# First batch of an attention + FFN kernel: plain value casts and plain products ahead of the dilated scores, a quarter of w_in in three loads, and a new order for the third FFN tile's first products

## The chip, the cores and the metric

One core of one Trainium2 chip. The metric is the device time of one launch in microseconds (us), as the median over runs. The engines that the text speaks of are PE (TensorE: matmuls, with its weight loads shown as PEld), DVE (VectorE), ACT (ScalarE), POOL (GpSimd, which here mostly issues loads) and SP (SyncE, which issues loads, transposing transfers and stores).

## The reference

Two stages. Attention over 8 batches, 8 heads, 576 tokens and head size 64, in which heads 0 to 3 ("plain") see the last 32 tokens, and heads 4 to 7 ("dilated") see every fourth token of the last 128:

```python
scores = scale * np.matmul(q, k.transpose(0, 1, 3, 2))
mask_plain = (rel >= 0) & (rel < window)
mask_dil = (rel >= 0) & (rel < window * dilation) & (rel % dilation == 0)
attn = np.exp(scores); attn = attn / (np.sum(attn, axis=-1, keepdims=True) + 1e-09)
attn_out = np.matmul(attn, v)
```

Then a feed-forward network on the 4608 tokens, each a row of 512 (8 heads x 64):

```python
h = np.maximum(x @ w_in, 0.0)          # 512 -> 2048
out = h * h @ w_out                    # 2048 -> 512
```

## The kernel before

**Tiling.** Heads go in pairs e = 0 to 3; pairs 0 and 1 are plain, 2 and 3 dilated. Tokens are kept by residue modulo 4. The attention's result goes, transposed and in bf16, into a ring `xT` (partitions: 128 of the 512 features, so four k-blocks `kt`, one for each head pair). The FFN takes tokens in tiles of 512; the first two tiles are made as four half tiles of 256. In a tile the first layer accumulates in PSUM over the four k-blocks (`mm1`, L971), ScalarE takes the relu (L984), VectorE squares (L987); the second layer (`g2`, L1026) multiplies by `w_out`. A half tile's accumulator holds two of the sixteen blocks of 128 hidden features, a full tile's one. The pool `ps_f` has four PSUM buffers, shared by the first layer's accumulators, the second layer's outputs and some scores.

**What orders the work.** Nothing is scheduled by a planner: each engine runs its instructions in the order in which the program issues them, and waits where its operands or its buffer aren't ready. That order is written out by hand in the string `PROGRAM`. Its first part, up to the first `|`, runs ahead of the FFN; each later part runs after one FFN group (`ffn_groups` gives the groups, `g1` those of the first layer). For batch 0, part 0 (the first 256 tokens) and part 1 (the other 320) of pair e, a code is a letter, e and the part:

- `T` PE transposes q and k into PSUM (L794), `C` copies them to SBUF, on ACT for a code that ends in a, else on DVE (L801 for dilated pairs, with a second copy at L803 for part 1; L808 and L809 for plain ones)
- `B` puts the mask's bias into PSUM (L824), `S` the scores (L846), `E` the exponential on ACT (L854), in part 1 with a mask multiplied in on DVE (L857)
- `P` products with the values (L884), `D` the sums that normalise (L900), `L` and `X` their reciprocal as log and exponential on ACT (L907, L910), `M` the division into `xT` on DVE (L917). In part 0 L, X and M take both pairs at once: L00, X00, M00 for the plain ones, L20, X20, M20 for the dilated
- `w` and `W` are zero products (`turn`, L764) of 512 and 256 columns, which keep PE running while it would wait; `w1+31` is one that adds into S31's accumulator
- `N` zeroes halves of the values' tile `vbd` on DVE (L1047, L1048); `h` casts the plain values of the first four blocks of 64 tokens from float32 into it on DVE (L1139; SP loads them at the start, L1065); `j` casts the dilated tail (L1142); `G` spreads dilated values into `vbd` (L245); `u` makes masks on ACT
- `L0:i0` loads a quarter of w_in, `L0:i1a` and `L0:i1b` halves of the second quarter (k-blocks 0 and 1, 2 and 3), `L0:v1s` and `L0:v1t` plain values of part 1, `L0:o0` to `o3` w_out: all issued on POOL's queue

**POOL's queue.** Its loads share eight semaphores in turn, so each waits, ahead of its issue, until the load eight before it has landed.

**The FFN's first groups.** In the first half tile a group of `g1` covers two accumulators and two k-blocks: group 0 and 1 use w_in's first quarter, 2 and 3 its second. The dilated pairs' `xT` blocks (k-blocks 2 and 3) are first read in group 1. In the third tile (tokens 1024 to 1535) the k-blocks come in the order 2, 3, 1, 0, and the first four groups issue the sixteen products of the first four accumulators in an order of their own.

Of the kernel before, what the change touches and what calls it, by code (L numbers as in the profile page):

```python
# [18 lines left out]


PROGRAM = (
# [42 lines left out]
def kernel(  # L64
# [29 lines left out]
    NT = 512  # L94
# [7 lines left out]
    KT = DM // P  # L102
# [826 lines left out]
    def store(osb, pos: int, c0: int, c1: int, cuts=None):  # L929

        x = 0
        while x < P:
            b, y = divmod(pos + x, S)
            part = int(y >= RES * MN[0]) if b in PARTED else 0
            w = MN[part] if b in PARTED else M
            r, m = divmod(y - RES * MS[part], w)
            n = min(P - x, w - m)
            row = b * S + RES * (MS[part] + m) + r
            at = cuts(n) if cuts else (c0, c1)
            for y0, y1 in zip(at, at[1:]):  # L940
                nc.sync.dma_start(out[row : row + RES * (n - 1) + 1 : RES, y0:y1], osb[x : x + n, y0:y1])
            x += n

    def ffn_groups(tk0: int, nt: int):

        early = NT <= tk0 <= 3 * NT
        h2 = h2_pool.tile([P, NF, NT], bf16, name="h2T")
        per = NT // nt  # L950
        kts = (2, 0, 3, 1) if tk0 > 3 * NT else (2, 3, 1, 0) if tk0 == 2 * NT else (0, 1, 2, 3) if tk0 == 0 else (2, 3, 0, 1)
        cur, acc = {}, {}

        half = nt // 2
        over = tk0 // RING != (tk0 + nt - 1) // RING
        assert not over or (tk0 + half) % RING == 0

        def mm1(u, ks):
            if u not in acc:
                acc[u] = ps_f.tile([P, NT], f32, name="pf")  # L960
            for x in range(per):
                f = per * u + x
                piece = max(y for y in range(len(w_in_sb)) if w_cuts[y] <= P * f)
                c0 = 512 * (f // 4) + f % 4 - w_cuts[piece]
                for kt in ks:
                    t0 = tk0 % RING
                    to, rhs = acc[u][:, nt * x : nt * x + nt], xT[:, kt, t0 : min(t0 + nt, RING)]
                    if over:
                        to = to.rearrange("p (a t) -> p a t", a=2)
                        rhs = xT[:, kt, :].rearrange("p (a t) -> p a t", t=half)[:, 0 : t0 // half + 1 : t0 // half, :]  # L970
                    nc.tensor.matmul(  # L971
                        to,
                        w_in_sb[piece][:, kt, c0 : c0 + 509 : 4],
                        rhs,
                        start=(kt == kts[0] and x == 0),
                        stop=(kt == kts[-1] and x == per - 1),
                        skip_group_check=True,
                    )
            if ks[-1] != kts[-1]:
                return  # L980
            hv = h2[:, per * u : per * u + per, 0:nt]

            def relu():
                nc.scalar.activation(hv, acc[u][:, :].rearrange("p (x n) -> p x n", x=per), ACT.Relu)  # L984

            def square():
                nc.vector.tensor_tensor(out=hv, in0=hv, in1=hv, op=ALU.mult)  # L987

            def floor():
                nc.vector.tensor_scalar(  # L990
                    out=hv, in0=acc[u][:, :].rearrange("p (x n) -> p x n", x=per), scalar1=0.0, scalar2=None, op0=ALU.max
                )

            if tk0 == 0 and u < 2:
                held.append((floor if u else relu, square))
            else:
                relu()
                square()

        def g1(i):  # L1000
            if i < 2 and tk0 < NT or i < 6 and tk0 == 0:
                x, y = divmod(i, 2)
                for ks in [kts[2:3], kts[3:]] if tk0 and y else [kts[2 * y : 2 * y + 2]]:
                    for u in (2 * x, 2 * x + 1):
                        mm1(u, ks)
            elif i < 2 and early:
                for u in (2 * i, 2 * i + 1):
                    mm1(u, kts[:2])
            elif i < 4 and tk0 == 2 * NT:
                for u, x in ((0, 2), (1, 2), (2, 2), (0, 3)) if i == 2 else ((1, 3), (3, 2), (2, 3), (3, 3)):  # L1010
                    mm1(u, kts[x : x + 1])
            elif i < 4 and early:
                for u in (2 * i - 4, 2 * i - 3):
                    mm1(u, kts[2:])
            else:
                mm1(i, kts)

        def g2(m, part):
            last = tk0 + P * (m + 1) == NTOK
            if part == 0 or last and part == 2:  # L1020
                cur[m] = ps_f.tile([P, DM], f32, name="pf")

            c0, c1 = ((0, 384), (384, DM))[part // 2] if last else (0, DM)
            f0, f1 = (NF // 2 * (part % 2), NF // 2 * (part % 2 + 1)) if last else (4 * part, 4 * part + 4)
            for f in range(f0, f1):
                nc.tensor.matmul(  # L1026
                    cur[m][:, c0:c1], h2[:, f, P * m : P * m + P], w_out_sb[:, f, c0:c1],
                    start=(f == 0), stop=(f == NF - 1),
                )
            if f1 == NF:  # L1030
                osb = osb_pool.tile([P, DM], f32, name="osb")
                (nc.vector.tensor_copy if last and part == 1 or tk0 == 3 * NT // 2 else nc.scalar.copy)(osb[:, c0:c1], cur[m][:, c0:c1])  # L1032
                pos = tk0 + (P * m + half) % nt if over else tk0 + P * m
                if tk0 == NTOK - NT and m in (0, 2):
                    store(osb, pos, c0, c1, lambda n: (c0, DM // 2, c1) if m == 0 or n > P // 2 else (c0, c1))
                else:
                    store(osb, pos, c0, c1)

        return [lambda i=i: g1(i) for i in range(NF // per)] + [
            lambda m=m, part=part: g2(m, part) for m in range(nt // P) for part in range(4)  # L1040
        ]
# [58 lines left out]

    def load_w_in(x, half=""):

        ks = {"": slice(0, KT), "a": slice(0, KT // 2), "b": slice(KT // 2, KT)}[half]
        nc.gpsimd.dma_start(
            w_in_sb[x][:, ks, :],
            moe_w_in[P * ks.start : P * ks.stop, w_cuts[x] : w_cuts[x + 1]].rearrange("(kt p) f -> p kt f", p=P),
        )
# [191 lines left out]
```

## Time and profile before

| | |
|---|---|
| median of 3 runs | 296.63 us (296.29 to 296.87) |
| the profiled execution | 296.3 us, span 294.3 us |
| PE busy | 289.2 us, 98% of the span |
| ACT, DVE, POOL busy | 64%, 53%, 42% |
| granted TensorE clock | 0.998 |

The span runs from the first to the last instruction in the trace; 2.0 us of the profiled time lie outside it. Rows of a timeline give the start in us from the span's start, the time from the first instruction's start to the last one's end, engine, line, operation, what is written and read, shapes, and how many instructions are merged in the row; in brackets the idle time before it and what ended that. A matmul's end is modelled and overlaps with the next one's start, so distances between starts are the better measure. A row of the table by stretches gives the stretch, its length, then for PE, PEld, DVE, ACT and POOL the busy time and the number of instructions, then granted clock, DMA share and GB/s.

### The profile page before, as it was taken

Reading aid. Unit: us, or ns where it says so; the run is one execution under the profiler, and the core shown is the slowest. Engines: PE = TensorE matmul, PEld = TensorE weight load, DVE = VectorE, ACT = ScalarE, POOL = GpSimd, SP = SyncE. Lnnn points to the kernel's source line nnn. Section 1 sums busy time; section 2 is a strip of 40 time slices with the busy share of each in tenths; the row PEclk is TensorE's granted clock in tenths of the full one; section 3 lists DMA queues with packets and bytes.
Section 4 is the critical chain, followed back from the end, with each engine's and each line's share of the span. In section 5 each row is a group of like instructions: output and inputs, shape, how many; then the busy total and the mean of one; then the engine's idle time right before and its main releaser. Section 6 shows DMA issues by size and latency. Waiting matters only on the chain.

```text
span 294.3 us, 7986 instructions
## 1 busy us (share of the span) xinstructions
PE 289.2 (98%) x3273; PEld 167.0 (57%) x3273; DVE 155.1 (53%) x449; ACT 187.7 (64%) x382; POOL 123.2 (42%) x208
## 2 busy tenths in 40 slices
PE   8999999999999999999999999999999999999995
PEld 7689647859555554555455545554554455445443
DVE  2786225646669666785659465947454244004400
ACT  6888635887767774988577656766676466127511
POOL 8676266666647959365873688000000000000000
PEclk9999999999999999999999999999999999999999
DMA  8999999999999999989999699012101210121022
GB/s 120 196 185 210 205 217 195 176 178 171 177 219 145 142 203 165 129 134 167 171 175 137 91 146 174 7 36 74 36 2 39 72 38 0 36 74 36 0 71 74
DMA packets 82996, 35.48 MB, mean 121 GB/s; under 512 B 52384, under 2 KB 78208, under 8 KB 82960
## 3 DMA queue, kind: packets, MB, share of 16 engines
q0 software_dynamic: 49056, 18.49, 56.6%
q1 hardware_dynamic: 33760, 16.38, 28.0%
q8 instruction: 26, 0.43, 0.6%
q10 hardware_dynamic: 144, 0.10, 0.1%
q14 instruction: 10, 0.08, 0.1%
HBM read 37.50 MB, written 9.44 MB: 159 GB/s over the span
## 4 chain that ended last, share of the span: by engine, by line
PE 98%; ACT 0%; issue 0%; DVE 0%; ACTq 0%
PE pf L1026 43%; PE pf L971 43%; PE po L764 2%; PE po L369 2%; PE pa L369 1%; PE pf L369 1%; PE pa L794 1%; PE pd L369 1%; PE pf L846 1%; PE pa L564 0%; PE po L884 0%; PE pf L824 0%; PE pd L900 0%; PE pf L564 0%; PE pf L884 0%
## 5 line engine op out<-in xcount | busy, mean ns | idle before, releaser
L971 PE MATMUL pf<-xT,w_in 128*128 128x512 bf16 (+1 forms) x704 | 127.9, 341 | 0.0
L1026 PE MATMUL pf<-w_out_sb,h2T 128*128 128x512 bf16 (+2 forms) x592 | 127.8, 373 | 0.0
L984 ACT ACTIVATE h2T<-pf 128x512 bf16<-128x512 f32 x143 | 83.9, 600 | 32.2 <-PE pf L971 31.9
L971 PEld LDWEIGHTS <-w_in 128*128 128x128 bf16 x704 | 78.0, 113 | 46.3 <-issue 0.3
L987 DVE TENSOR_TENSOR h2T<-h2T 128x512 bf16<-128x512 bf16 x144 | 60.1, 424 | 62.6 <-ACT h2T L984 60.5
L1026 PEld LDWEIGHTS <-h2T 128*128 128x128 bf16 x592 | 56.1, 98 | 63.9
L323 POOL DMA_DIRECT2D vbd<-in_v_dram x80 | 43.6, 553 | 22.8 <-DMA qb<-in_q_dram 8.6
L1032 ACT COPY osb<-pf 128x512 f32<-128x512 f32 (+1 forms) x34 | 19.5, 574 | 50.5 <-PE pf L1026 50.5
L173 POOL DMA_DIRECT2D qb<-in_q_dram x19 | 13.6, 720 | 10.4 <-DMA xx<-qb 7.3
L713 ACT ACTIVATE rec<-rec 128x576 f32<-128x576 f32 x24 | 16.4, 682 | 0.7
L173 POOL DMA_DIRECT2D kb<-in_k_dram x19 | 13.3, 699 | 6.0 <-DMA vd<-in_v_dram 1.8
L195 POOL DMA_DIRECT2D vbd<-in_v_dram x16 | 10.9, 679 | 10.6 <-DMA kb<-in_k_dram 4.8
L730 ACT ACTIVATE pt<-pa 128x384 bf16<-128x384 f32 (+1 forms) x26 | 11.7, 498 | 4.7 <-DVE xT L720 3.8
L309 POOL DMA_DIRECT2D vd<-in_v_dram x20 | 12.0, 614 | 2.7 <-DMA vbd<-in_v_dram 1.6
L716 DVE TENSOR_TENSOR xT<-pf,rec 128x512 bf16<-128x512 f32 x11 | 7.6, 692 | 10.5 <-ACT rec L713 10.5
L315 POOL DMA_DIRECT2D vbd<-in_v_dram x20 | 12.0, 622 | 1.6 <-PE pf L369 1.6
L716 DVE TENSOR_TENSOR xT<-po,rec 128x512 bf16<-128x512 f32 x13 | 9.0, 691 | 6.4 <-ACT rec L713 6.2
L732 DVE TENSOR_TENSOR pt<-pt,mask_f 128x384 bf16<-128x384 bf16 x24 | 8.4, 355 | 6.2 <-ACT pt L730 6.1
L732 DVE TENSOR_TENSOR pt<-pt,mask_n 128x384 bf16<-128x384 bf16 (+1 forms) x20 | 7.2, 374 | 8.5 <-ACT pt L730 8.4
L337 DVE COPY qT<-xx 64x576 bf16<-64x576 bf16 (+1 forms) x30 | 10.8, 360 | 0.6
L369 PEld LDWEIGHTS <-vbd 64*64 64x64 bf16 x328 | 8.3, 107 | 4.2 <-issue 3.7
L730 ACT ACTIVATE pt<-pf 128x448 bf16<-128x448 f32 (+1 forms) x18 | 8.6, 519 | 0.7 <-PE pf L369 0.6
(160 smaller groups left out, 283.3 us busy)
## 6 DMA issues: line engine op xcount, KB each, us to landing
qb<-in_q_dram POOLq DMA_DIRECT2D x7, 320.0 KB, 7.2
kb<-in_k_dram POOLq DMA_DIRECT2D x7, 320.0 KB, 8.6
vd<-in_v_dram POOLq DMA_DIRECT2D x34, 64.0 KB, 4.7
w_out_sb<-in_moe_w_out_dram POOLq DMA_DIRECT2D x4, 512.0 KB, 13.4
out_dram<-osb SPq DMA_DIRECT2D x16, 128.0 KB, 5.0
qb<-in_q_dram POOLq DMA_DIRECT2D x6, 256.0 KB, 7.5
kb<-in_k_dram POOLq DMA_DIRECT2D x6, 256.0 KB, 7.9
out_dram<-osb SPq DMA_DIRECT2D x9, 160.0 KB, 5.3
```

The source lines that it names most:

```text
L173: nc.gpsimd.dma_start(t[p0 : p0 + n, part, h0:h1, :], src[b, h0:h1, t0 : t0 + RES * n, :].rearrange("h (p r) d -> p h (r d)", r=RES),)
L323: nc.gpsimd.dma_start(v_rows[b % 2][p0 + 16 * r : p0 + 16 * r + 16, e, :, :], v[b, 2 * e + hl, :, :].rearrange("(i m r) d -> r m i d", r=R ...
L369: nc.tensor.matmul(out, lhs, rhs, start=begin, stop=True, skip_group_check=True)
L713: nc.scalar.activation(rec[:, :], rec[:, :], ACT.Exp, scale=-1.0)
L716: nc.vector.tensor_tensor(out=tok[:, :, 16:M], in0=byr(o[:, :]), in1=byr(rec[:, 0:512]), op=ALU.mult)
L730: nc.scalar.activation(pt, sp[b, e][g][:, 0:n], ACT.Exp, scale=SCALE)
L732: nc.vector.tensor_tensor(out=pt, in0=pt, in1=mask, op=ALU.mult)
L971: nc.tensor.matmul(to, w_in_sb[piece][:, kt, c0 : c0 + 509 : 4], rhs, start=(kt == kts[0] and x == 0), stop=(kt == kts[-1] and x == per - ...
L984: nc.scalar.activation(hv, acc[u][:, :].rearrange("p (x n) -> p x n", x=per), ACT.Relu)
L987: nc.vector.tensor_tensor(out=hv, in0=hv, in1=hv, op=ALU.mult)
L1026: nc.tensor.matmul(cur[m][:, c0:c1], h2[:, f, P * m : P * m + P], w_out_sb[:, f, c0:c1], start=(f == 0), stop=(f == NF - 1),)
L1032: (nc.vector.tensor_copy if last and part == 1 or tk0 == 3 * NT // 2 else nc.scalar.copy)(osb[:, c0:c1], cur[m][:, c0:c1])
```

## The change

Three edits.

1. In `PROGRAM` code `h` moves from behind C30v to right behind `N`, so ahead of C20v on DVE. P00, P10, D00, D10 and L00 move from behind G30 to right behind C30v, so ahead of S20 and E20; X00 and M00 move ahead of C31a; `j` moves from behind M00 to behind M20. The zero products `W1 w1` that stood behind `h` go.
2. `L0:i1b` becomes `L0:i1c` and `L0:i1d`, one k-block each; group 3 of the first half tile multiplies k-block 2 for both accumulators, then k-block 3. (Before, it did both k-blocks of one accumulator, then of the other.)
3. In the third tile the first sixteen products are issued in a new order. Written as accumulator and place of the k-block, before: 00 01 10 11 | 20 21 30 31 | 02 12 22 03 | 13 32 23 33. After: 00 01 10 11 | 20 21 02 12 | 22 30 31 32 | 03 13 23 33.

```diff
 PROGRAM = (
-    "L0:q001 L0:q023 L0:q123 L0:v0d L0:i0 L0:q101 L0:v1d L0:i1a L0:i1b L0:v1s L0:i2a L0:v1t L0:i2b L0:i3 L0:o0 L0:o1 "
-    "L0:o2 L0:o3 L1:q00123 y L1:q10123 L1:v0dp s28x183 T00 C00a T10 C10a B00 B10 w1 S00 E00 B20 W1 S10 E10 N u B30 W1 "
-    "w1 T20q w1 T20k C20v T30 C30v h W1 w1 S20 E20 w1 S30 E30 T21 C21v T31 C31a G20 G30 P00 P10 D00 D10 L00 X00 P20 "
-    "P30 D20 D30 L20 X20 M00 j S21 S31 w1+31 M20 E21 E31 G21 G31a | T01q T11q | T01k C01v T11k C11a r P21 P31 D21 D31 "
+    "L0:q001 L0:q023 L0:q123 L0:v0d L0:i0 L0:q101 L0:v1d L0:i1a L0:i1c L0:i1d L0:v1s L0:i2a L0:v1t L0:i2b L0:i3 L0:o0 "
+    "L0:o1 L0:o2 L0:o3 L1:q00123 y L1:q10123 L1:v0dp s28x183 T00 C00a T10 C10a B00 B10 w1 S00 E00 B20 W1 S10 E10 N h u"
+    " B30 W1 w1 T20q w1 T20k C20v T30 C30v P00 P10 D00 D10 L00 S20 E20 w1 S30 E30 T21 C21v T31 X00 M00 C31a G20 G30 "
+    "P20 P30 D20 D30 L20 X20 S21 S31 w1+31 M20 j E21 E31 G21 G31a | T01q T11q | T01k C01v T11k C11a r P21 P31 D21 D31 "
...
         def g1(i):
             if i < 2 and tk0 < NT or i < 6 and tk0 == 0:
                 x, y = divmod(i, 2)
-                for ks in [kts[2:3], kts[3:]] if tk0 and y else [kts[2 * y : 2 * y + 2]]:
+                for ks in [kts[2:3], kts[3:]] if (tk0 or x == 1) and y else [kts[2 * y : 2 * y + 2]]:
                     for u in (2 * x, 2 * x + 1):
                         mm1(u, ks)
+            elif i < 4 and tk0 == 2 * NT:
+                for u, x in ((0, 0), (0, 1), (1, 0), (1, 1), (2, 0), (2, 1), (0, 2), (1, 2),
+                             (2, 2), (3, 0), (3, 1), (3, 2), (0, 3), (1, 3), (2, 3), (3, 3))[4 * i : 4 * i + 4]:
+                    mm1(u, kts[x : x + 1])
             elif i < 2 and early:
                 for u in (2 * i, 2 * i + 1):
                     mm1(u, kts[:2])
-            elif i < 4 and tk0 == 2 * NT:
-                for u, x in ((0, 2), (1, 2), (2, 2), (0, 3)) if i == 2 else ((1, 3), (3, 2), (2, 3), (3, 3)):
-                    mm1(u, kts[x : x + 1])
             elif i < 4 and early:
...
-        ks = {"": slice(0, KT), "a": slice(0, KT // 2), "b": slice(KT // 2, KT)}[half]
+        ks = {"": slice(0, KT), "a": slice(0, 2), "b": slice(2, KT), "c": slice(2, 3), "d": slice(3, KT)}[half]
```

## The prediction

> **What bounds the kernel now.** I read the page first, for the whole span.
>
> ```profile
> span 294.3 us, 7986 instructions
> PE 289.2 (98%) x3273; PEld 167.0 (57%) x3273; DVE 155.1 (53%) x449; ACT 187.7 (64%) x382; POOL 123.2 (42%) x208
> q8 instruction: 26, 0.43, 0.6%
> ```
>
> TensorE (PE) is busy for 98%, so a change here is worth what it takes from PE's row, and nothing else. The third line is the fetching of instructions: 0.43 MB in 26 packets, against PE's 2 x 3273 = 6546 instructions, is 66 bytes each and 252 instructions a packet. That queue brings PE's program in blocks.
>
> The first 15 us are short matmuls, and zero products (L764) fill waits there, so "busy" is no proof of useful work. The timeline of PE, in order of time (start, length, count):
>
> ```profile
> 9.65 0.50 PE L764 MATMUL po<-kbd 128*128 128x256 bf16 x2
> 10.08 0.31 PE L846 MATMUL pf<-xx 64*64 64x64 bf16 x8
> 10.32 0.39 PE L764 MATMUL po<-kbd 128*128 128x512 bf16 x1
> 10.64 0.31 PE L846 MATMUL pf<-xx 64*64 64x64 bf16 x8
> 10.88 0.34 PE L794 MATMUL pa<-mk,qb 80*64 80x80 bf16 x8
> ...
> 11.58 0.49 PE L884 MATMUL pf<-pt,vbd 128*128 128x96 bf16 x8
> 11.90 0.48 PE L900 MATMUL pf<-pt,ones 128*128 128x96 bf16 x8
> 12.31 0.44 PE L884 MATMUL po<-pt,vd 64*64 64x64 bf16 x16
> ...
> 13.32 0.18 PE L846 MATMUL pf<-xx 64*64 64x32 bf16 x1
> 14.01 0.45 PE L846 MATMUL pf<-xx 64*64 64x32 bf16 x15 [0.50 <-issue]
> ...
> 14.65 1.04 PE L971 MATMUL pf<-xT,w_in 128*128 128x256 bf16 x8
> ```
>
> Starts are what to read, since ends overlap. The one idle of PE here is inside S31: its first matmul starts at 13.32, the next at 14.01, 0.69 later, and the releaser is "issue", no engine and no load. I counted instructions around it, in stretches (PE and PEld counts):
>
> ```profile
> 9.15:13.40 4.25, 4.25 (x129) 3.22 (x128) 3.12 (x10) 3.39 (x10) 3.19 (x5) 1.00 1.32 201
> 13.40:14.00 0.60, 0.10 (x7) 0.01 (x1) 0.52 (x2) 0.60 (x2) 0.00 (x0) 1.00 1.45 196
> 14.00:20.55 6.55, 6.54 (x127) 5.70 (x128) 5.19 (x14) 5.51 (x14) 4.81 (x7) 1.00 1.45 192
> ```
>
> From 9.15 to the stall PE ran 257 instructions, one block (the seven matmuls of the middle row started before it). The DMA view of 11.50 to 12.60 has this line, that of 0 to 11.50 none:
>
> ```profile
> q8 instruction: 1, 0.02, 5.5%
> ```
>
> My reading: entering a block at 9.15 asks for the next one; its packet moves after 11.50 behind the loads, and PE, which needs it at 13.3, gets it at 14.0. Both the request (9.15) and the traffic ahead of it lie before anything that the change touches. That is an inference from one stall.
>
> **The change, part by part.** *Filler out, products forward.* PE loses one pair of zero products (9.65 to 10.08, 0.43 us) and P00 P10 D00 D10 come in its place. By the starts above: P 0.32, D 0.41, S20 0.24, filler 0.32, S30 0.24, the four transposes of T21 and T31 0.70 (10.88 to 11.58). From 9.65 this puts S20 at 10.38 instead of 10.08, S30 at 10.94, the transposes at 11.18, P20 at 11.88 instead of 12.31, and S31 at 12.9 instead of 13.32 at the earliest: 0.43 early. What these need:
>
> ```profile
> 8.09 0.48 DVE L1048 MEMSET vbd<- 64x512 uint32 x1
> 9.51 0.76 DVE L801 COPY xx<-pa 128x512 bf16<-128x512 bf16 x2 [0.94 <-PE pa L794]
> 10.18 0.94 DVE L1139 CAST vbd<-osb 64x512 bf16<-64x512 f32 x2
> ```
> ```profile
> L1065 SPq DMA_DIRECT2D osb<-in_v_dram x4: 616/616/770, 0.8 to 2.9; - x4
> DMA to landing us min/median/max: 2.5/4.0/5.1
> ```
>
> The casts (code h) move ahead of C20v on VectorE. Their loads are there by 2.9 + 5.1 = 8.0, VectorE is free at 8.57, and 0.94 of casts fit the 0.94 us in which it now waits: they end at 9.51. P00 at 9.65 and C20v at 9.51 keep their places. If that cover is gone, each us that h is late delays P00, C20v and C30v alike; SyncE's queue is not changed. ScalarE pays:
>
> ```profile
> 10.43 0.38 ACT L854 ACTIVATE pt<-pf 128x256 bf16<-128x256 f32 x1 [0.30 <-PE pf L846]
> ...
> 11.69 0.69 ACT L801 COPY xx<-pa 128x640 bf16<-128x640 bf16 x1 [0.31 <-PE pa L794]
> 12.42 0.60 ACT L907 ACTIVATE rec<-pf 128x512 f32<-128x512 f32 x1
> 13.04 0.63 ACT L910 ACTIVATE rec<-rec 128x512 f32<-128x512 f32 x1
> ```
>
> Its order is now L00, E20, E30, X00, C31a. D10 starts its last product just before 10.38 and a short product takes 0.2, so from 10.5: 0.60 + 0.38 + 0.38 + 0.63 + 0.69 = 2.68, and C31a ends at 13.2 at the earliest, instead of 12.38. S31 reads that copy. It could have started at 12.9 and starts at 13.2 to 13.3, where it stands today. VectorE takes M00 ahead of the second half of C31, which waits for C31a anyway. So the 0.43 us of PE turn into a wait for ScalarE ahead of S31, and then comes the block at 14.0. Four instructions fewer stand ahead of the block's end, so two more matmuls of S31 run before it: 0.03 us gained at 14.65. X00 and M00 are done a full us sooner, but the first FFN product is not waiting for them alone: it follows S31 and one filler, and w_in's first quarter bounds it:
>
> ```profile
> 6.27 0.84 POOL L1104 DMA_DIRECT2D w_in<-in_moe_w_in_dram  x1
> ```
> ```profile
> DMA to landing us min/median/max: 7.7/7.7/7.7
> ```
>
> 6.27 + 7.7 = 13.97, so 14.65 can come forward by 0.68 at the most whatever happens. Between 0 and -0.68 I take -0.03, by the rows of the stall.
>
> [...]
>
> *w_in's second quarter in three loads.* POOL issues one load more; a load is issued when the one eight before it has landed, so the next eight issues each hang on a landing one later in the queue.
>
> ```profile
> 12.15 0.72 POOL L195 DMA_DIRECT2D vbd<-in_v_dram  x1
> 14.21 0.68 POOL L195 DMA_DIRECT2D vbd<-in_v_dram  x1 [1.33 <-DMA w_in<-in_moe_w_in_dram]
> ```
> ```profile
> 19.11 2.81 PE L971 MATMUL pf<-xT,w_in 128*128 128x256 bf16 x24
> ```
>
> These are the first two plain loads of part 1, and the second waits for w_in's first quarter. In the new order the first one does: 14.2 instead of 12.15, and those behind it follow later by an issue or so. The same bytes go in the same order through engines that are busy throughout (the DMA digit is 9), so landings stay. PE's 24 products from 19.11 take 2.81 / 24 = 0.117 each with no break, so the old second half had landed by 20.0, where the ninth, its first reader, starts; in the new order k-block 3 is read four products (0.47 us) later still. Cost 0: the queue of transfers that is already waiting hides the later issues. Without that cover a landing moves with its issue, and a product right behind it waits as long: +0.7 above (one issue), 0 below, since PE has no wait there to lose.
>
> *Third tile.* Sixteen products fill four accumulators; the fourth accumulator's buffer is freed by a copy on VectorE.
>
> ```profile
> 83.50 2.25 PE L971 MATMUL pf<-xT,w_in 128*128 128x512 bf16 x9
> 84.94 2.53 PE L971 MATMUL pf<-xT,w_in 128*128 128x512 bf16 x11
> ```
> ```profile
> 84.21 0.68 DVE L1032 COPY osb<-pf 128x512 f32<-128x512 f32 x1
> 86.44 0.60 ACT L984 ACTIVATE h2T<-pf 128x512 bf16<-128x512 f32 x1 [1.68 <-PE pf L971]
> ```
>
> One product takes (2.53 - 0.38) / 10 = 0.215; the seventh, at 84.94, should have come at 84.79: a wait of 0.15 for the copy that ends at 84.89. In the new order the fourth accumulator comes tenth, at 85.44, and the wait goes. But the first accumulator's last product moves from twelfth (86.02) to thirteenth (83.50 + 12 x 0.215 = 86.08), and the seventeenth product takes over its buffer. Today its relu follows 0.42 later, ends at 87.04, and the seventeenth starts at 87.10. In the new order the relu ends at 87.10 and the seventeenth starts at 87.16, though it could have at 86.94. So 0.15 is gained and 0.21 lost: +0.06. Bounds: -0.15 if the buffer comes free sooner, +0.21 if other work on ScalarE comes between.
>
> *Sum*: -0.03 + 0 + 0.06 = +0.03. The profiled execution took 296.3 us, 2.0 more than its span, and lies 0.3 under the median of the three timed runs, 296.63. So 296.33 profiled, 296.65 as a median. About 0.2%, 0.6 us, is what a measurement of this kernel can tell from no change.
>
> **The rivals.** *The stall goes.* If the 0.69 isn't a block that comes at its own time, S31 runs from 13.3 to 13.65, a filler follows, and the FFN starts at 14.0 to 14.05, just behind w_in's first quarter: -0.6. With +0.06 in the third tile that is -0.54, or -0.75 with its wait gone and no new one: 295.9 to 296.1. For it: "issue" names no cause, and there is one such stall only. Against: the count of 257 and the packet.
>
> *ScalarE becomes the bound, and the stall follows.* If the stall is a fixed 0.69 after the block's end is reached, and the pauses that ScalarE now has ahead of E20 and C31a (0.30 and 0.31 in the rows) recur behind the new L00, C31a ends at 13.8 to 13.9, S31 starts 0.6 later than today and the whole 0.69 comes on top: FFN at 15.2, +0.6, with the third tile +0.66: 297.3. It decides as soon as C31a ends past 13.4. If the block comes at 14.0 instead, this lateness is covered.
>
> **How the numbers follow.** No change 0.52 (296.4 to 296.9); the stall goes 0.29, of which 0.22 past the bound of 296.04 and 0.07 within it; ScalarE 0.19, of which 0.17 past 297.2 and 0.02 within. Faster 0.22, same 0.52 + 0.07 + 0.02 = 0.61, slower 0.17. The range from 295.9 to 297.2 holds the first two cases and leaves the third out.
>
> **What the new profile would show.** Right: P00 at 9.6 to 9.7 with no idle; C31a's end near 13.2; PE's "issue" idle still inside S31, two matmuls further, ending near 14.0; the first L971 at 14.6; no gap from 19.11 to 21.9; the fourth accumulator at 85.4 (shifted as the rest is), a short gap before the seventeenth product. Wrong: no "issue" idle and the first L971 near 14.0 (first rival); S31 past 13.8 with a stall behind it (second); or a wait on w_in in the products at 19 to 24 us, which would mean that landings did move with the issues.

## The result, and the profile after

| | before | after |
|---|---|---|
| median of 4 runs | 296.62 us (296.29 to 296.87) | 299.52 us (299.45 to 300.0) |
| ratio | | 1.0099 (95% interval 1.0079 to 1.0119) |
| profiled execution | 296.3 us, span 294.3 | 299.45 us, span 297.5 |
| granted TensorE clock | 0.998 | 0.994 |

The changed kernel is 2.9 us slower, where 296.65 was predicted. 36 later executions of the same kernel, in four runs of the experiments (e9, e12, e13, e14), were nearer: 296.6 to 299.3, median 297.8, with the kernel before at 296.6 to 296.7 beside them. So two things need a cause: the 1.1 us that came back, and the rest of the first 2.9. In what follows, ratios leave out a few executions of 301 us and more that ran in a slower state, which the medians hold, so a ratio isn't quite the quotient of two medians.

The timeline of PE after the change, for the stretch that the prediction quoted of before:

```profile
9.43 0.49 PE L884 MATMUL pf<-pt,vbd 128*128 128x96 bf16 x8
...
12.35 0.46 PE L846 MATMUL pf<-xx 64*64 64x32 bf16 x16
12.64 0.20 PE L846 MATMUL pf<-xx,kbd 64*64 64x64 bf16 x2
12.67 0.23 PE L846 MATMUL pf<-xx 64*64 64x32 bf16 x3
14.34 0.49 PE L846 MATMUL pf<-xx 64*64 64x80 bf16 x12 [1.44 <-issue]
...
15.28 1.92 PE L971 MATMUL pf<-xT,w_in 128*128 128x256 bf16 x8
```

P00 starts at 9.43 with no idle ahead of it. The "issue" idle is still inside S31, two matmuls further on (behind three, not one), and it still ends at about 14: 14.34. But PE is there at 12.7, so the idle has grown from 0.50 to 1.44 us. And the first eight FFN products behind it take 1.92 us instead of 1.04. The table by stretches (stretch, length, PE, PEld, DVE, ACT, POOL, granted clock, DMA share, GB/s) tells why:

```profile
12.70:14.30 1.60, 0.20 (x11) 0.08 (x5) 1.53 (x7) 1.47 (x3) 0.09 (x1) 1.00 1.36 191
14.30:17.80 3.50, 3.46 (x40) 2.24 (x41) 1.86 (x7) 1.40 (x3) 3.15 (x5) 0.53 1.32 200
```

For 3.5 us behind the idle the granted clock is 0.53. Of before, the same table has 1.00 behind its idle:

```profile
14.00:16.00 2.00, 1.99 (x42) 1.62 (x42) 1.94 (x6) 1.76 (x4) 1.41 (x2) 1.00 1.37 198
```

Lined up by their weight loads, the two traces drift apart in steps: PE goes on 0.33 us late at the idle (14.34 against 14.01), the second FFN group is 1.77 late (17.80 against 16.03; the 1.44 between the two is the low clock), less than 0.1 more until 58 us; then 0.8 at 70 us, 0.33 at 80, and 0.05 in the third tile; 3.2 at the end. The step at 70 us is a row of the chain of waits after the change (start, length, what), the last transposing transfer of batch 2's q:

```profile
58.45 10.34 DMA xx<-qb
```

Before it was issued at 56.24 and took 7.0 us. PE then waits for a copy behind that transfer:

```profile
70.35 0.33 PE L369 MATMUL pa<-xx 64*64 64x80 bf16 x14 [0.61 <-DVE qT L278]
```

My first theory was a chain: the block behind the border inside S31 comes at its own time; PE, now early, idles 1.4 us; the idle lowers the clock; the slip of 1.8 us makes batch 2 late.

### The profile page after: what moved, and what is told of

Read it like the earlier page. It is cut to its first block, busy times and chain, and to the rows that moved or that the text cites. A ratio compares the mean times of both kernels' runs of the same rounds, so it can differ in the third digit from the quotient of the medians.

```text
span 297.5 us, 7954 instructions
## 1 busy us (share of the span) xinstructions
PE 288.3 (97%) x3243; PEld 166.8 (56%) x3271; DVE 153.9 (52%) x449; ACT 187.5 (63%) x382; POOL 123.6 (42%) x209
## 4 chain that ended last, share of the span: by engine, by line
PE 90%; DMA 5%; issue 1%; POOL 1%; DVE 1%; ACT 0%; ACTq 0%; POOLq 0%
PE pf L971 42%; PE pf L1027 39%; DMA xx<-qb 3%; DMA kb<-in_k_dram 2%; PE po L369 2%; PE pa L369 1%; PE pf L369 1%; PE pd L369 1%; PE pa L794 1%; PE pf L846 1%; PE pa L564 0%; POOL qb L173 0%; PE po L884 0%; PE pd L900 0%; PE pf L564 0%
## 5 line engine op out<-in xcount | busy, mean ns | idle before, releaser
L1027 PE MATMUL pf<-w_out_sb,h2T 128*128 128x512 bf16 (+2 forms) x571 | 126.1, 373 | 1.7 <-issue 0.8
L173 POOL DMA_DIRECT2D kb<-in_k_dram x19 | 13.4, 703 | 5.5 <-DMA w_in<-in_moe_w_in_dram 2.1
```

Of the source, the lines that this page charges most:

```text
L173: nc.gpsimd.dma_start(t[p0 : p0 + n, part, h0:h1, :], src[b, h0:h1, t0 : t0 + RES * n, :].rearrange("h (p r) d -> p h (r d)", r=RES),)
L1027: nc.tensor.matmul(cur[m][:, c0:c1], h2[:, f, P * m : P * m + P], w_out_sb[:, f, c0:c1], start=(f == 0), stop=(f == NF - 1),)
```

## The experiments

Each ran beside the kernel before, on the same chip.

**Where the block's border lies.** Three kernels, each the changed one with one place of `PROGRAM` altered, move the border or fill the time in front of it. e1 has five more zero products of 512 columns ahead of S30; e2 has 86 small zero products of 64x16 (a new code `k`) in place of 14 of the warm-up's 28; e3 has 8 such small products behind the warm-up.

```diff
-S20 E20 w1 S30 E30
+S20 E20 w6 S30 E30
```
```diff
-s28x183
+s14x183 k86
```
```diff
-s28x183
+s28x183 k8
```

> The changed kernel with six zero products instead of one ahead of S30: 10 instructions and some 1.07 us of PE work more ahead of the point where PE stood idle. Theory 'block and clock' (PE reaches the end of an instruction block early, the next block comes at its own time near 14.3, the idle of 1.44 us lets the granted clock fall): the 'issue' idle shrinks to about 0.4 to 0.6 us, stays five instruction pairs earlier in the program, the granted clock stays at 1.0 from 14 to 18 us, the first FFN product starts near 14.7 to 15.0 at full speed, and the time is that of the kernel before, 296.4 to 297.2. Rival 'order' (the new order on ScalarE and VectorE makes the FFN's operands late): the filler adds to it or is hidden, 299.5 to 300.5, the slow products stay. Rival 'loads' (the extra load): unchanged, 299.5.

> The changed kernel with 144 instructions more in the warm-up of PE and about the same time there: 14 zero products of 183 columns and 86 of 16 columns instead of 28 of 183. Only the places where blocks of 256 instructions end move, 144 instructions towards the start of the program. 'Block and clock': the block that held PE up is asked for before 5 us and needed near 11; the idle inside S31 goes, the clock stays at 1.0, the first FFN product starts at 14.0 to 14.4 (w_in's first quarter), and the time is 295.5 to 296.6, under the kernel before. Rivals 'order' and 'loads': nothing that they blame has changed, 299.5.

> The changed kernel with eight zero products of 16 columns more in the warm-up, 16 instructions. 'Block and clock': the 'issue' idle stands 16 instructions, so eight matmuls, earlier in the program, that is ahead of the last matmuls of S21 and not in S31, ends at about the same 14.3, and the slow products and the time stay (299 to 300). A stall that waits for an operand or a buffer of S31 would stay at S31's third or fourth matmul.

Measured: e1 300.47 us (298.43 to 301.06; ratio 1.0124, 1.0083 to 1.0165), e2 301.54 (ratio 1.0162, 1.0133 to 1.019), e3 297.62 in one execution. In none of the three traces is there an idle inside S31, and the clock stays at 1.00 behind it. But e2 and e3 got there in a way that I hadn't meant: PE runs at half speed until 17.6 us in e2 and until 10.2 in e3, so it comes to the border after the block. In e3 the small products need not be the reason, since e5 below, with the usual warm-up, is at half speed until 10.5. And e1's traced execution, without stall and without low clock, took 298.43, two others at a mean clock of 1.00 took 300.0 and 300.9, where the theory had 296.4 to 297.2; but 1.07 us of that is the work that e1 adds. So the chain can't be the whole cause. As tests of the border e2 and e3 failed; as a test of "stall and clock are the loss", e1 spoke against it, though its slower executions have no trace.

**The loads and the third tile, in the old order of the first batch.** e4 is the changed kernel with the `PROGRAM` of before, but for the one code that names the loads:

```diff
-L0:i1b
+L0:i1c L0:i1d
```

> The kernel before with two of the three edits: w_in's second quarter in three loads, and the third tile's order; the order of the first batch is the old one. 'Block and clock' and 'order': as the kernel before, with the 0.06 us of the third tile, 296.5 to 296.9. 'Loads': most of the 2.9 us, 298.5 to 299.5.

Measured: e4 296.61 us against 296.38, ratio 1.0005 (0.9986 to 1.0023): no difference that this run can tell. I took it as "the loads cost nothing", which was too much for an interval that reaches to +0.7 us; its own trace had a wait of 0.52 for w_in at 24.5 us and one of 0.82 for w_out at 38.4 us, and I put them down to that execution.

**The order alone; the border moved without small products; a slip without the new order.** e5 is the kernel before with the new `PROGRAM`, but for the loads, which stay. e6 is the changed kernel and e7 the kernel before with 10 long zero products as the warm-up. e8 is the kernel before with nine zero products behind S31 instead of one.

```diff
-L0:i1c L0:i1d
+L0:i1b
```
```diff
-s28x183
+s10x512
```
```diff
-w1+31
+w9+31
```

> The kernel before with the new order of the first batch alone: w_in's second quarter stays one load, the third tile keeps its order. Theory (the instruction block arrives at its own time, a longer idle in front of it lowers the clock, the slip puts batch 2's transposes behind later loads): the order carries all of the loss but the 0.06 of the third tile, so 299.4 (299.0 to 299.8). Rival (the loss needs the extra load on POOL's queue, which shifts later issues): 296.6 to 297.2.

> The changed kernel, but the warm-up's 28 zero products of 183 columns are 10 of 512: the same columns (5124 and 5120) in 18 products fewer, so every border of a 256-instruction block comes 18 products later in the program, behind S31, in the first FFN products. Order, data and work of all other engines as in the changed kernel. Theory: PE reaches the border only near 14 to 14.5, when the block is there or nearly so; the idle shrinks from 1.44 to under 0.6 us, the clock stays at 1.00 and the time falls by 1.3 us or more: 296.3 to 298.2. Rival (the loss is from the new order on ScalarE and VectorE, or from the loads): the time stays at 299.2 to 299.8.

> The kernel before with the same 10 long zero products in place of 28. Theory: the stall of 0.69 inside S31 goes or shrinks behind it, so 296.0 to 296.6, or no change if the block comes later by as much as its border. Rival (the stall is not a block's border): it stays inside S31 at the same matmul, 296.6.

> The kernel before with 8 more zero products behind S31 (nine in place of one), which delay the FFN by 8 x 0.213 = 1.70 us and change nothing ahead of it. Theory (a slip of 1.8 us at the FFN's start lets batch 2's transposes fall behind later loads, which costs another 1.2 us from 70 to 85 us): 296.6 + 1.7 + 0.8 to 1.2 = 299.1 to 299.5, with a wait for batch 2's transposes near 70 us. Rival (the later losses belong to the new order, not to the slip): 298.3, and no such wait.

Measured: e5 296.9 (295.63 to 299.12; ratio 1.0, 0.9969 to 1.0031), e6 297.16 (ratio 1.0023, 0.9996 to 1.0049), e7 297.0 (1.0018, 0.9995 to 1.004), e8 298.66 (1.0063, 1.0044 to 1.0082), with 296.67 of before. On e5 the theory missed, and the rival's 296.6 to 297.2 holds the median: the order by itself carries no loss in the median. On e6 the theory's time and clock held. e8 is nearer to the rival's 298.3 than to the theory's 299.1. In e8 the FFN is 1.73 us late as meant, the copy behind batch 2's transposes waits,

```profile
67.32 0.19 DVE L345 COPY kbd<-xx 64x128 bf16<-64x128 bf16 x1 [2.25 <-DMA xx<-qb]
```

and yet PE has no wait behind it: the shift is 1.73 at the first FFN product and 1.75 at the end. A slip of that size isn't enough for the loss at 70 us; that link of the chain fell. The traces of e5 and e18 lose 0.3 and 0.4 us at the same copy (L278), e18 with an FFN that is only 0.2 us late: all three have the new order, but no run takes this apart.

The border, though, is shown. In e6, with 18 products fewer ahead of it, the idle moves out of S31 to exactly 18 products further on, among the first FFN products, and in e7 too:

```profile
14.15 0.41 PE L971 MATMUL pf<-xT,w_in 128*128 128x256 bf16 x2 [0.43 <-DMA w_in<-in_moe_w_in_dram]
15.08 0.84 PE L971 MATMUL pf<-xT,w_in 128*128 128x256 bf16 x6 [0.52 <-issue]
```

The trace gives the time of each packet of the instruction queue. In all sixteen traces with an idle at the border, those of later runs too, PE goes on 2.2 to 2.5 us after the packet starts; ten of them:

| | packet | PE goes on | | packet | PE goes on |
|---|---|---|---|---|---|
| before | 11.59 | 14.01 | e8 | 11.49 | 14.01 |
| after | 12.03 | 14.34 | e9 | 11.29 | 13.56 |
| e4 | 11.91 | 14.25 | e10 | 11.21 | 13.52 |
| e6 | 12.59 | 15.08 | e11 | 11.60 | 13.82 |
| e7 | 13.38 | 15.80 | e18 | 11.29 | 13.56 |

The time of packets is the first column of their records in the trace, PE's the first product behind the border. e7 also tells that an idle nearly as long as the result's doesn't have to lower the clock. Between 14.21 and 15.80 PE starts nothing (1.58 us, against 1.64 in the result's trace; the profile counts 1.19 and 1.44 of them as idle, and names a VectorE copy in e7, which had ended), and behind it the clock is 1.00:

```profile
14.30:15.80 1.50, 0.31 (x2) 0.01 (x2) 1.44 (x4) 1.47 (x4) 0.94 (x2) 1.00 1.37 190
15.80:19.60 3.80, 3.80 (x72) 3.23 (x72) 2.52 (x8) 2.18 (x6) 3.39 (x6) 1.00 1.42 190
```

**The parts side by side on one chip.** The changed kernel again (e9); order and loads with the old third tile (e10), which undoes this part of the change; the order alone again (e11, as e5).

```diff
-            elif i < 4 and tk0 == 2 * NT:
-                for u, x in ((0, 0), (0, 1), (1, 0), (1, 1), (2, 0), (2, 1), (0, 2), (1, 2),
...
+            elif i < 4 and tk0 == 2 * NT:
+                for u, x in ((0, 2), (1, 2), (2, 2), (0, 3)) if i == 2 else ((1, 3), (3, 2), (2, 3), (3, 3)):
...
```

> The changed kernel once more, unaltered, beside the two that follow, on one chip. The order alone took 296.9 (ten runs from 295.6 to 299.1), the loads with the third tile 296.6, so the two parts don't add up to 299.5. Theory (all of it hangs on when PE reaches the block's border in an execution: early, and the idle passes 1.2 us and lowers the clock; late, and there is no stall): a wide spread with both kinds, median 297.0 to 299.5, lowest under 297. Rival (order and loads together make a loss that neither makes alone): all runs within 299.2 to 300.2, as in the first four.

> The changed kernel with the third tile's old order, so the new first batch and the three loads of w_in's second quarter. Theory: as the changed kernel, 0.06 lower. Rival (order and loads together): as the changed kernel, and 2 to 3 us above the order alone.

> The order alone once more, beside the two above. Theory (the loads cost nothing): the same median as with the loads, within 0.5. Rival (order and loads together): 296.9 again, 2 to 3 us under the kernel with the loads.

Measured, against 296.64 of before: e9 298.0 (296.63 to 299.25; ratio 1.0043, 1.0021 to 1.0065), e10 297.41 (1.003, 1.0012 to 1.0048), e11 296.42 (0.9996, 0.9976 to 1.0016). So the loss is real, it is smaller than in the result, and within the new order it comes with the loads. In the traces of e9 and e10 PE is early (the first FFN product at 14.17 and 14.12, against 14.65 before) and loses 0.37 and 0.25 us of that at 22 us, by plain values of part 1 that the extra load has pushed back; the row of e9:

```profile
22.18 0.36 PE L884 MATMUL pa<-pt,vbd 128*128 128x96 bf16 x5 [0.21 <-DMA vbd<-in_v_dram]
```

e11 has no such wait. These two executions, of 296.73 and 296.33 us, end no later than before. Theory and rival each held in part: the executions spread, and the loads do cost, but 1 to 1.6 us above the order alone, not 2 to 3.

**More traces of the two unaltered kernels.**

> The changed kernel, unaltered, for one more trace. Its time varies by execution (296.6 to 300.0 in sixteen). Theory: the trace tells the time by three lengths before the second FFN group: the idle at the block's border, the length of PE's slow start, and the waits for part 1's values at 19 to 22 us. An execution of 298 or more at full clock shows either a slow start that lasts past 9 us, or waits for values or transposes at 19 to 24 and 60 to 85 us of 1 us or more in all. Rival: its loss is spread evenly over the FFN, and none of these differs.

> As the run before it: the same kernel, another execution, the same three lengths.

> As the two runs before it: the same kernel, another execution, the same three lengths.

> The kernel before, unaltered, for a second trace on the same chip as the three looks at the changed kernel. Theory: the block's packet is followed by the first product behind the border 2.2 to 2.5 us later, as in the first trace, and an idle at the border stays under 1 us; 296.0 to 297.5.

Measured, with 296.68 of before: e12 297.74 (ratio 1.0026, 1.0003 to 1.0049), e13 297.94 (1.0033, 1.0007 to 1.0059), e14 297.38 (1.0016, 0.9995 to 1.0038); e15, the kernel before, 296.97 (1.0022, 0.9997 to 1.0047), which tells how far such a median moves by itself. e15 came as expected; the theory on the changed kernel missed, as e12's 298.45 at full clock has neither a long slow start nor 1 us of waits at 19 to 24 and 60 to 85 us. All three traces of the changed kernel show the idle at the border at 0.77 to 0.91 us, ending at 13.81 to 14.31, with the clock at 1.00. What they have and no trace of the old loads has are waits further on, at the same two places in each. From e12, weight loads at 23.9 us and second-layer products at 37.4:

```profile
23.89 1.13 PEld L971 LDWEIGHTS <-w_in 128*128 128x128 bf16 x11 [0.37 <-DMA w_in<-in_moe_w_in_dram]
```
```profile
37.41 2.32 PE L1027 MATMUL pf<-w_out_sb,h2T 128*128 128x512 bf16 x10 [0.28 <-DMA w_out_sb<-in_moe_w_out_dram]
```

Against the trace of before the shift grows by 0.29 and 0.43 us at these two places in e12, 0.30 and 0.70 in e13, 0.32 and 0.15 in e14, and by nothing at either place in e15, e11 or the order-alone kernel with the third tile (e17, next). Not every trace with the extra load has them: e2, e3, e6, e9, e10 and the result's own have neither (e9 and e10 wait at 22 us instead), though e6's FFN is about as early (0.24 us late).

The rest of what e12 and e14 lose lies at the very end. From PE's last weight load to the end of the span it is 3.7 to 3.8 us in fifteen of the twenty traces, but 4.8 in e12, 5.0 in e14, 4.9 in e17, 4.3 in e9 and in e11. In e12, e14 and e17 the last packet of PE's instruction queue falls among the packets of the last store, 1.2 us behind the last copy, and the store's last landing comes about 1 us late; from e12, the view of the instruction queue from 293.4 to 294.6 us:

```profile
q8 instruction: 1, 0.02, 5.2%
```

e11 and e17 have no extra load, so this isn't its doing. All five have the new order, and none of the six traces of the old order shows it; whether the order brings it is open.

**The two halves of the answer.** e16 is the kernel before with the three loads of w_in's second quarter and the order of group 3 that goes with them; e17 is the changed kernel without these two.

```diff
-L0:i1b
+L0:i1c L0:i1d
```
```diff
-L0:i1c L0:i1d
+L0:i1b
```

> The kernel before with w_in's second quarter in three loads and nothing else. Theory (the extra load puts each later issue on POOL's queue behind a landing one later, so that w_in's third quarter lands 0.5 to 0.9 us later near 24 us and the last of w_out 0.7 to 1.4 us later near 37 us, and PE, which reads them as they land, waits there): 296.9 to 297.8, with waits of 0.3 to 0.8 us in all on w_in and w_out. Rival (the loads cost nothing in the old order, since PE is later there): 296.4 to 296.8 and no such waits.

> The changed kernel with w_in's second quarter in two loads, as before: the new order of the first batch and of the third tile stay. Theory (the loads carry most of the excess that repeats, the order none, the third tile 0.05): 296.5 to 297.0, no wait on w_in or w_out from 20 to 40 us. Rival (the loss needs order and third tile, not the loads): 297.6 to 298.2, as the changed kernel.

Measured, with 296.51 of before: e16 297.3 (ratio 1.0016, 1.0000 to 1.0032), e17 296.52 (1.0007, 0.999 to 1.0025). Both times lie in the theory's ranges; the two intervals overlap, though, and e17's twelve executions fall into eight from 296.0 to 296.7 and four from 297.6 to 297.8. The traced one is of the four, and its 1.1 us is the late end just described. The trace of e16, the old order with the new loads, has the two waits:

```profile
23.87 1.24 PEld L971 LDWEIGHTS <-w_in 128*128 128x128 bf16 x12 [0.40 <-DMA w_in<-in_moe_w_in_dram]
```
```profile
37.83 1.89 PE L1026 MATMUL pf<-w_out_sb,h2T 128*128 128x512 bf16 x8 [0.71 <-DMA w_out_sb<-in_moe_w_out_dram]
```

They shift it by 0.33 and 0.87 us, more than the 0.3 to 0.8 in all that the theory had. The view of the loads of w_out on POOL's queue, of their last two or three, before and then in e16 (the last line is the time from issue to landing):

```profile
L1110 POOL DMA_DIRECT2D w_out_sb<-in_moe_w_out_dram x3: 544/548/558, 20.6 to 21.6; - x3
...
DMA to landing us min/median/max: 12.4/13.4/14.4
```
```profile
L1110 POOL DMA_DIRECT2D w_out_sb<-in_moe_w_out_dram x2: 533/562/591, 20.6 to 21.7; - x2
...
DMA to landing us min/median/max: 13.6/14.8/16.1
```

The last is issued at the same time, 21.6 and 21.7, and lands at 36.0 and 37.8, the moment at which PE goes on. So it isn't a later issue that makes w_out late, as the theory had it; the transfers take longer. The other traces that tell this landing have it at 35.6 to 36.3 us with the old loads (e7, e8, e17, e18) and at 36.1 to 38.1 with the new ones (after, e1, e2, e3, e6, e9, e10, e12, e14), so 1.8 us is near the top of a range that starts at next to nothing. Why one load more for the same bytes does that isn't settled here.

**The order without its wait.** A last kernel moves the border 12 products forward in e11's kernel.

```diff
-s28x183
+s40x128
```

> The kernel before with the new order of the first batch (no extra load, old third tile), and the warm-up's 28 zero products of 183 columns as 40 of 128: nearly the same columns (5124 and 5120) in 12 products more, so every block's border comes 12 products earlier in the program. Theory (a block is asked for when the one before it is entered, and PE goes on 2.2 to 2.5 us after its packet starts): PE enters the block earlier, so the packet starts 0.3 to 0.5 us earlier, and the idle now falls ahead of S31 or in S21 and ends near 13.4 to 13.8: 296.2 to 296.6 at 0.0 to 0.4 under the order alone (296.4 to 296.9). Rival (the packet comes when the traffic lets it, whatever the entry): the idle is longer by what PE reaches the border earlier, it ends at 13.8 to 14.1 again, and the products behind the border come later: 296.6 to 297.2.

Measured: 296.79 against 296.54, ratio 1.0006 (0.9991 to 1.0021). The packet comes at 11.29 (e11: 11.60) and the first FFN product at 14.37, 0.28 before that of the kernel before. But PE stands again ahead of 19.76, and the gain is gone:

```profile
19.76 0.96 PE L971 MATMUL pf<-xT,w_in 128*128 128x256 bf16 x7 [0.30 <-DVE xT L917]
```

The profile names the division into `xT`, which ended at 19.60; but in before, e9, e10, e11 and e17 the same product starts 0.3 us before that division ends. What fits is the next border: this product is the 128th behind the first border, and it follows the next packet, at 17.36, by 2.40 us. PE entered the block 1.0 us earlier than in e11 and the packet came 0.3 earlier; but among executions of the changed kernel that packet comes anywhere from 11.29 to 12.03, so the 0.3 can't be told from chance. The idle ended at 13.56, where the theory had it; the time lies in the rival's range. No kernel that ran is faster than the one before by more than a measurement can tell.

## Why the prediction was wrong

Two steps failed, one in the result's own executions and one in the later ones.

**"So the 0.43 us of PE turn into a wait for ScalarE ahead of S31, and then comes the block at 14.0 … I take -0.03"**: in the result's trace this term is +1.77 at the second FFN group. PE wasn't held by ScalarE: it reached the block's border at 12.7, stood 1.44 us, went on 0.33 late, and then ran 3.4 us at half clock, which cost 1.44. That trace loses another 1.15 from 70 to 80 us, for which the sum had no term. The cause of the 2.9 us stays open beyond that one trace: of the result's other three executions, two had a mean clock of 0.989 and 0.988, but one had 1.00 and took 299.47 all the same.

**"The same bytes go in the same order through engines that are busy throughout, so landings stay … Cost 0"**: this is the step that failed in the later executions. The landings moved. The upper end that was named there, +0.7 for one issue, was about the size (0.3 and 0.4 us of waits in e12, 1.2 in all in e16's trace; 0.8 between the medians of e16 and before), and a wait on w_in at 19 to 24 us, seen at 23.9 in e12 and e16, was among the prediction's signs of being wrong. The cover that the text trusted, PE without a wait from 19.11 to 21.9, did hold for the second quarter of w_in. What came late was what is loaded behind it: w_in's third quarter, the plain values of part 1, the last of w_out. For their readers the working had nothing but "landings stay".

**"PE, which needs it at 13.3, gets it at 14.0"**: the mechanism was right. The idle is a block's border: it moved two matmuls within S31 as said, 18 products with 18 products, and PE follows the packet by 2.2 to 2.5 us in sixteen traces. That the time is pinned was right only within limits: 13.5 to 14.6 us for the unmoved border, by execution. So the first rival, that the stall goes, fell. The crossing costs 0.1 to 1.4 us of PE's idle in these sixteen traces, in which PE reaches the border before the packet is 2.2 to 2.5 us old.

**"C31a ends at 13.2 at the earliest"**: wrong, by 0.65 us. ScalarE after the change:

```profile
10.26 0.60 ACT L907 ACTIVATE rec<-pf 128x512 f32<-128x512 f32 x1 [0.53 <-PE pf L900]
10.76 0.70 ACT L854 ACTIVATE pt<-pf 128x256 bf16<-128x256 f32 x2
11.35 0.62 ACT L910 ACTIVATE rec<-rec 128x512 f32<-128x512 f32 x1
11.87 0.68 ACT L801 COPY xx<-pa 128x640 bf16<-128x640 bf16 x1
```

L00 began 0.24 earlier than worked out, since PE itself was 0.22 earlier (P00 at 9.43, not 9.65), and the five instructions took 2.29 us from the first start to the last end, their starts and ends overlapping, against 2.68 as separate terms. So S31 had no wait for ScalarE, the second rival (C31a past 13.4) never came near, and all of PE's lead became idle at the border. In the later executions this changed nothing that can be told, as the border absorbs it either way: e5, e11 and e17 have 296.9, 296.42 and 296.52 against 296.67, 296.64 and 296.51. In the result's trace the longer idle was followed by the low clock.

**Third tile, +0.06**: right, in its mechanism too. The shift against before grows by 0.05 us over it in after, e9, e12, e13, e14 and e17, and by 0.00 in e11, which keeps the old order. In after the wait ahead of the seventh product is gone (1.30 us behind the first, 1.44 before), and the seventeenth starts 3.65 behind the first instead of 3.60.

**What no step had**: the fall of the clock to 0.53, about 1.4 us of the first trace. An idle that grows was priced by its end alone. Whether the idle caused it is open: it followed 1.64 us without a start there, didn't follow 1.58 us in e7, and in 36 later executions of the changed kernel a mean clock of 0.994 came four times (298.1 to 299.2 us), in 146 of the kernel before 0.992 to 0.994 came five times (297.4 to 299.0, and once 304.8); three of the result's four executions had 0.994 or less. In the trace's record of the clock the fall comes 10.24 us after the rise (4.25 us) and lasts 3.41; the full clock behind it lasts 279.89, that of before 286.72; 10.24, 279.89 and 286.72 are 3, 82 and 84 times 3.413. What makes the clock fall at 14.48 and not in e7 isn't shown.

Open as well is the 0.8 us at 70 us, of which e5's trace shows 0.3 and e8's, with the same slip, nothing. The 0.33 us at 80 is, by its place, another block border: from the product at 14.34 to the one at 79.98 PE's records after the change have 2048 instructions (1022 products, as many weight loads, 4 semaphore instructions), eight times 256. There e1, e3, e5, e10, e11 and e12 lose 0.16 to 0.64 us at the very same count of PE's products, with 1245 ahead, though e1's and e3's programs have five and eight products more before it, and there PE goes on 2.4 to 3.2 us after a packet. So a lead that survives the first border can still be lost at a later one.

So the two sizes of the loss have different makings. Of the 1.1 us of the 36 executions the extra load is half or a little more (0.5 by e16's ratio, 0.8 by its median). Their four traces, e9, e12, e13 and e14, end 0.5, 2.2, 1.4 and 1.5 us later than the trace of before; of that 0.40, 0.73, 1.02 and 0.48 is waits for loads from 22 to 38 us, and 0.48, 1.02, 0.02 and 1.23 the late end. The executions that the ratios use, as means over the kernel before on the same chip, give +0.4 us for the loads in the old order (e4, e16), +0.1 for the new order without them (e5, e11, e17) and +0.95 for both (e9, e10, e12 to e14), each good to about 0.3: order and loads may cost more together than apart, which these runs can't decide. The 2.9 us of the result are, by its one trace, 0.33 at the border, 1.44 of low clock, 0.82 at a copy behind batch 2's late transfer, 0.33 at the later border and 0.05 in the third tile, with 0.2 in small steps; PE is so late there that the loads of w_in and w_out are in time, and the extra load doesn't show. That larger loss was seen in four executions and not again.

## What to carry to other kernels

When a transfer is split ahead of a long queue of others, price the readers of everything behind it, not those of the split transfer: here the split load itself was never waited for. Work moved ahead of an instruction block's border only lengthened the wait at that border here, and in e18 at the next one; look for the packet of the instruction queue and for the engine's idle some 2.3 us behind it. And where executions of one kernel differ by more than the change, an interval of a single run is too narrow: the median of four was 1.7 us above that of 36 later ones.

## What the runs showed of the hardware

- PE's stream comes in packets of 16 KB (0.43 MB in 26), one for 257 instructions by the count in before, for 256 by that of eight blocks in after (2048); at the first border PE goes on 2.2 to 2.5 us after the packet's start at the earliest, and idled 0.1 to 1.4 us there in the sixteen traces in which it arrived sooner.
- The granted clock was 0.50 for 3.41 us after an idle of 1.44 us in the result's trace, and 1.00 behind one of 1.19 us in e7. The row of the result's trace:

```profile
14.48:17.89 3.41, 3.41 (x41) 2.19 (x38) 1.68 (x7) 1.40 (x3) 3.24 (x5) 0.50 1.32 199
```

- PE was at half speed at the start. In before, the 28 products of 183 columns that begin at 1.07 us last until the next start at 5.47, 0.86 ns a column, against 0.42 in the third tile (0.215 us for 512). The trace's record of full clock begins at 3.9 to 7.1 us in most traces, at 10.2 and 10.5 in e3 and e5, and at 17.6 in e2, which has small zero products of 64x16 for half of the warm-up. Two products of 256 columns took 0.85 us in e2 there, against 0.50 of before at 9.65, while the table gives a granted clock of 1.00: half speed at the start doesn't show in that column, only in the durations. From e2, the timeline and the table:

```profile
11.72 0.85 PE L764 MATMUL po<-kbd 128*128 128x256 bf16 x2
```
```profile
10.00:14.00 4.00, 4.00 (x53) 2.10 (x54) 1.98 (x5) 2.42 (x8) 2.40 (x4) 1.00 1.30 197
```

- With one load split in two, for the same bytes, a load that is issued eleven places later landed 1.8 us later in e16's trace than in that of before, though it was issued at the same time; in nine other traces with the extra load it landed 0.1 to 2.1 us later than in the trace of before.
